# Splitting weights in pairs, combining from PSUM, and scaling O later: one transformer block on one core

## The chip, the core and the metric

The kernel runs on one core of a Trainium2 chip. A core has a matrix engine (PE; its weight loads are shown as PEld), a vector engine (DVE), a scalar engine (ACT) and GpSimd (POOL). They run at the same time, each working through its own queue in order, and wait for each other by semaphores. SyncE (SP) does no arithmetic; its queue issues the transfers between the core's memory (SBUF) and the chip's memory (HBM), which 16 DMA engines carry out. PE writes to PSUM, eight banks of 128 x 512 float32 values; DVE and ACT read and write PSUM and SBUF, POOL only SBUF.

The metric is the device time of one execution in microseconds (us). The time before is the median of three runs. The profile is that of one execution, with a time of its own.

## The reference

One block: a layer norm scaled and shifted by a condition c, attention of 32 query heads over a cache of 16 key/value heads, of which only the last 512 positions count, an output projection, a second such norm, and a gated feed-forward network. 2048 tokens of width 576, head size 128, hidden size 4608, all float32.

```python
mod = (_silu(c) @ w_mod).reshape(c.shape[0], 6, 1, -1)
sa, ca, ga, sb, cb, gb = (mod[:, 0], mod[:, 1], mod[:, 2], mod[:, 3], mod[:, 4], mod[:, 5])
h = _layernorm(x, axis=-1) * (1 + ca) + sa
x = x + ga * _A_ref(h, A_k_cache, A_v_cache, A_wq, A_wo)
h = _layernorm(x, axis=-1) * (1 + cb) + sb
x = x + gb * _B_ref(h, B_w_gate, B_w_up, B_w_down)
...
q = (lambda x, *d: x.transpose(*d))((x @ wq).reshape(B, Sq, Hq, Dh), 0, 2, 1, 3)
scores = jnp.einsum("bhqd,bhkd->bhqk", q, k) * (Dh ** -0.5)
p = _softmax(scores, axis=-1)
o = jnp.einsum("bhqk,bhkd->bhqd", p, v)
```

## The kernel before

**Split numbers.** A float32 value v is kept as hi, a rounded form that PE takes (fp32r), and lo = v - hi. ACT makes hi by a copy, DVE or POOL subtracts to get lo. A matrix product is then three: hi times hi, hi times lo and lo times hi.

**Seven products for eight.** The big projections use the Strassen-Winograd scheme. x and the weights are cut into four quarters each, and combinations of quarters enter seven products. In the code the weight's factors are A11, A12, A22, S1, S2, S4, S3 and the activation's B11, B21, T1, T2, B22, T3, T4; product (u, A11) multiplies A11 by B11, A12 by B21, S1 by T1, S2 by T2, S4 by B22, S3 by T3 and A22 by T4.

**The Q phase.** The 2048 tokens are four blocks of 512. A pair of blocks (0 and 1, then 2 and 3) is the one halving of the scheme; the 576 input rows give the other (288 rows: two chunks of 128 and one of 32), and heads are taken two at a time. There are 32 units u: u 0 to 15 take the heads in order for blocks 0 and 1, u 16 to 31 again for blocks 2 and 3. Each unit has seven products, so the phase has 224 steps; `order` lists them, `place` gives a product's step, and step numbers begin at NLO = -224, so that attention begins at 0. One product is seven matmuls of 512 columns (`q_product`): for each 128-row chunk hi by hi, lo by hi and hi by lo, and one matmul for the 32-row chunk, which keeps hi and lo on different partitions.

The schedule is by step: `at_n(step, fn)` puts work before the step's product and `at_late` behind it. Each engine executes its own work in the order in which the program lists it.

- Weights: `load_raw(u)` fetches the four quarters of a unit into one of two RAW tiles (five transfers). `w_sums` has POOL form S1, S2, S4 and S3. `w_split` makes hi (ACT, 128 x 384) and lo (DVE, once 128 x 256 and once 32 x 128) of one factor, into one of nine `sw` tiles.
- First products: products A11 and A12 need only block 0. So for the first EARLY = 8 units these come ahead of everything, in the phase's first 16 steps, with their own loads (`load_first`) and splits (`w_split_first`); the A11 products are kept in `first_room`, tiles of blocks 2 and 3 that are not loaded yet. Meanwhile block 1 goes through its norm and the combinations T1 to T4 are made (`first_sum`, `chunk_split`). The early units' other five products follow unit by unit, and load the raw weights again.
- Outputs: each unit gives four tiles of 128 x 512, scaled by QSCALE, in one of four `qo` tiles, stored to HBM by SP (`q_store`). Sums of products are built in PSUM where the order allows; otherwise DVE adds a kept product (`q_out` with add). PSUM banks: a (two), b (one), c (one), st (four).
- The pair switch: while units 8 to 15 run, blocks 2 and 3 are loaded and normalised, transposed by PE (`turn`), copied with gain and shift (`third_out`), combined (`third_sum`), and kept in float32. When the last product of unit 15 with an old factor is issued, `convert` splits the new one into the same tile.
- Background work: `SPANS` and the planner loop behind it place jobs that prepare the later weights ("ab": load, four sums on POOL, store; "tail": load, sums, splits, 24 stores; "wo" and "down" likewise) in rooms that are free in certain steps. They run through the Q phase and attention.

**Attention.** 128 blocks b of four steps; each step handles 128 queries: scores (three matmuls; DVE takes the row maximum, `neg`), exponentials on ACT (`pp`), four transposes (`pt`), hi and lo of the transposed P (`ptt`, ACT and DVE), and three matmuls with V (`pv`, bank `ot`, two banks). The sums of a block's exponentials are inverted (`rs`), and since a row is needed that holds them along the free axis on every partition, they go through HBM: `put_rs` writes rs to rscr (2 KB), `get_rs` reads it back to all partitions as `rb` (256 KB), with SP waiting for the write to land. In step 4b+8, when the last matmul of the block's pv is issued, DVE multiplies O by rb into `ov`. `put_o` stores it two steps later; for some heads POOL first forms sums of O (`sum_o`, `put_sx`, `sum_last`).

After attention come the output projection and the feed-forward network, which the change leaves as they are.

Of the kernel before, what the change touches and what calls it, by code (L numbers as in the profile page):

```python
# [44 lines left out]
def adaln_block_kernel(ctx: ExitStack, tc: tile.TileContext, x, k_cache, v_cache, wq, wo, w_gate, w_up, w_down,  # L45
# [65 lines left out]
    def sw_tile(shape, dt=F32R):  # L111
        return qw.tile(shape, dt, tag="sw", name="sw", bufs=9)
# [125 lines left out]
    QC = {}  # L238

    def q_room(c):  # L240
        QC[c] = wp.tile([P, 5, BLK], F32R, tag=f"hc{c}", name="qc", bufs=1)

    def q_places(c, s):
        r, to = (slice(0, P), 3 + s) if s < 2 else (slice(TQ, 2 * TQ), 2)
        return r, QC[c][:, s, :], QC[c][r, to, :]

    def q_hi(c, s, v, k=None):
        hi = q_places(c, s)[1]
        if k is None:
            nc.scalar.activation(hi, v, AF.Copy)  # L250
        else:
            nc.scalar.activation(hi, v, AF.Identity, bias=scol[:, k : k + 1])

    def q_lo(c, s, v, eng, k=None):
        r, hi, lo = q_places(c, s)
        if k is None:
            eng.tensor_sub(lo, v[r], f32(hi[r]))
        else:
            eng.scalar_tensor_tensor(lo, v[r], scol[r, k : k + 1], f32(hi[r]), op0=OP.add, op1=OP.subtract)
# [26 lines left out]
    EARLY = 8  # L286
    wqh = wq.rearrange("(h r) n -> r h n", h=2)

    def load_raw(u):
        raw, n0 = RAW[u % 2], u % HKV * 2 * P  # L290
# [17 lines left out]
    def raw_of(u, a):  # L308
        return RAW[u % 2][:, :, {A11: 0, A21: 1, A12: 2, A22: 3}[a], :]

    def w_sums(u, which):
        for a in which:
            WS[u, a] = qw.tile([P, 3, P], F32, tag="ws", name="ws", bufs=5)
            eng = nc.gpsimd
            if a == S1:
                eng.tensor_add(WS[u, a], raw_of(u, A21), raw_of(u, A22))
            elif a == S2:
                eng.tensor_sub(WS[u, a], WS[u, S1], raw_of(u, A11))
            elif a == S3:
                eng.tensor_sub(WS[u, a], raw_of(u, A11), raw_of(u, A21))  # L320
            else:
                eng.tensor_sub(WS[u, a], raw_of(u, A12), WS[u, S2])

    def w_split(u, a, src=None):
        if src is None:
            src = raw_of(u, a) if (u, a) not in WS else WS[u, a]
        t = SWQ[u, a] = sw_tile([P, 5, P])
        nc.scalar.activation(t[:, 0:3, :], src, AF.Copy)
        nc.vector.tensor_sub(t[:, 3:5, :], src[:, 0:2], f32(t[:, 0:2, :]))
# [1496 lines left out]
```

## Time and profile before

| | |
|---|---|
| median of three runs | 3252.54 us (3252.29 to 3254.05) |
| the profiled execution | 3254.14 us, span 3252.3 us |
| mean granted clock of PE | 0.974 |
| moved by the DMA engines | 635.14 MB, 195 GB/s on average |

A profile row names line, engine and operation, then out<-in by the program's tile names, the shape, the count, the busy time, the mean time of one in ns, and the engine's idle time just before, with what ended it. All instructions have line L36 here, that of a helper through which every operation passes, so one goes by tile names: `a`, `b`, `c`, `st`, `pt` and `ot` are PSUM banks, `qc` the split activations of the Q phase, `sw` split weights, `ws` their sums, `raw` raw weights, `x` the blocks or whatever background work uses their room. `a<-qc,sw` is a matmul of a Q product. A window's row gives its length, the busy time of PE, PEld, DVE, ACT and POOL with counts, the granted clock as a fraction of full speed, the mean busy share of the DMA engines, and GB/s. In a list of waits, "A <- B: 131.9, 47, 7.8" means that A stood idle 131.9 us in all, 47 times, 7.8 us at the longest, until B was done. SPq is the queue of SP.

### The profile page before, as it was taken

Reading aid. Unit: us, or ns where it says so; the run is one execution under the profiler, and the core shown is the slowest. Engines: PE = TensorE matmul, PEld = TensorE weight load, DVE = VectorE, ACT = ScalarE, POOL = GpSimd, SP = SyncE. Lnnn points to the kernel's source line nnn. Section 1 sums busy time; section 2 is a strip of 40 time slices with the busy share of each in tenths; the row PEclk is TensorE's granted clock in tenths of the full one; section 3 lists DMA queues with packets and bytes.
Section 4 is the critical chain, followed back from the end, with each engine's and each line's share of the span. In section 5 each row is a group of like instructions: output and inputs, shape, how many; then the busy total and the mean of one; then the engine's idle time right before and its main releaser. Section 6 shows DMA issues by size and latency. Waiting matters only on the chain.

```text
span 3252.3 us, 50928 instructions
## 1 busy us (share of the span) xinstructions
PE 3023.0 (93%) x16375; PEld 2579.5 (79%) x16375; DVE 2323.0 (71%) x4113; ACT 1814.1 (56%) x3727; POOL 1846.8 (57%) x1680
## 2 busy tenths in 40 slices
PE   7897988788898889888999999999999999999999
PEld 5676776677777767667799999888888888888888
DVE  7878766676777767666878877766666686666667
ACT  5255446677777777666744465544444454444443
POOL 2645654577787777432155521776655565656555
PEclk9999998999999999999999999999999999999999
DMA  4664887888788877788644766655555565555554
GB/s 145 217 201 151 254 238 200 226 235 233 231 252 265 257 239 238 203 209 239 203 153 176 273 228 236 181 158 153 159 174 140 153 200 157 145 143 139 149 140 119
DMA packets 505386, 635.14 MB, mean 195 GB/s; under 512 B 55712, under 2 KB 425120, under 8 KB 496416
## 3 DMA queue, kind: packets, MB, share of 16 engines
q1 hardware_dynamic: 503984, 631.36, 65.0%
q8 instruction: 131, 2.15, 0.3%
q14 instruction: 135, 1.11, 0.1%
q10 hardware_dynamic: 1136, 0.53, 0.1%
HBM read 424.48 MB, written 207.25 MB: 194 GB/s over the span
## 4 chain that ended last, share of the span: by engine, by line
PE 58%; DMA 10%; issue 4%; DVE 3%; POOL 3%; SPq 2%; ACT 2%; DVEq 0%; POOLq 0%; ACTq 0%
PE a L36 19%; PE w L36 12%; PE c L36 10%; PE st L36 5%; PE b L36 5%; PE ot L36 5%; DMA rb<-rscr 4%; DMA rscr<-rs 4%; PE pt L36 3%; SPq L36 2%; DVE ptt L36 1%; POOL x L36 1%; DVE neg L36 1%; ACT pp L36 1%; POOL qt L36 1%
## 5 line engine op out<-in xcount | busy, mean ns | idle before, releaser
L36 DVE TENSOR_TENSOR x<-w,x 128x288 f32<-128x288 f32 x964 | 417.2, 451 | 233.5 <-PE w L36 231.3
L36 PE MATMUL a<-hc,sw 128*128 128x512 f32 x2016 | 580.4, 393 | 1.5 <-DVE v L36 1.4
L36 PE MATMUL st<-kt,qt 128*128 128x512 f32 x1536 | 504.6, 438 | 1.1 <-POOL qt L36 1.1
L36 DVE TENSOR_TENSOR ptt<-pt,ptt 128x512 fp32r<-128x512 f32 x512 | 351.6, 687 | 152.9 <-ACT ptt L36 152.1
L36 ACT ACTIVATE pp<-st,neg 128x512 f32<-128x512 f32 x512 | 352.1, 688 | 191.3 <-DVE neg L36 190.2
L36 PE MATMUL ot<-ptt,vs 128*128 128x512 f32 x1536 | 453.3, 404 | 4.8 <-DVE ptt L36 4.3
L36 PE MATMUL pt<-ident,pp 128*128 128x128 f32 x2048 | 323.3, 282 | 130.1 <-DVE ptt L36 125.4
L36 PEld LDWEIGHTS pt<-ident,pp 128*128 128x128 f32 x2048 | 260.2, 145 | 220.9 <-issue 126.4
L36 PEld LDWEIGHTS a<-hc,sw 128*128 128x128 f32 x2016 | 355.1, 188 | 41.5 <-DVE v L36 3.3
L36 POOL TENSOR_TENSOR qt<-qr,qt 128x512 fp32r<-128x512 f32 x128 | 165.5, 1293 | 371.7 <-ACT qt L36 354.1
L36 ACT ACTIVATE ptt<-pt 128x512 fp32r<-128x512 f32 x512 | 304.8, 595 | 115.4 <-PE pt L36 113.2
L36 ACT ACTIVATE sw<-sr 128x384 fp32r<-128x384 f32 x504 | 257.5, 518 | 188.3 <-issue 88.0
L36 PEld LDWEIGHTS ot<-ptt,vs 128*128 128x128 f32 x1536 | 296.4, 194 | 82.3 <-DVE ptt L36 12.9
L36 DVE TENSOR_REDUCE neg<-st 128x1 f32<-128x512 f32 x512 | 347.5, 679 | 2.7 <-PE st L36 2.7
L36 POOL TENSOR_TENSOR sw<-sr,sw 128x256 fp32r<-128x256 f32 x245 | 185.1, 756 | 275.4 <-ACT sw L36 256.9
L36 PEld LDWEIGHTS w<-wh,hl 128*128 128x128 f32 x1776 | 297.4, 188 | 53.2 <-DVE x L36 5.7
L36 PE MATMUL w<-wh,hl 128*128 128x288 f32 x1776 | 326.3, 295 | 3.0 <-DVE x L36 2.9
L36 PE MATMUL c<-hc,sw 128*128 128x512 f32 x1008 | 302.4, 393 | 0.0
L36 DVE TENSOR_TENSOR sw<-sr,sw 128x256 fp32r<-128x256 f32 x259 | 189.1, 731 | 142.7 <-ACT sw L36 140.0
L36 PEld LDWEIGHTS st<-kt,qt 128*128 128x128 f32 x1536 | 263.1, 198 | 28.0 <-POOL qt L36 2.1
L36 PE MATMUL a<-qc,sw 128*128 128x512 f32 (+1 forms) x912 | 238.4, 407 | 46.1 <-DVE qo L36 28.3
L36 POOL TENSOR_TENSOR hl<-vs,hl 128x512 fp32r<-128x512 f32 x139 | 192.0, 1382 | 107.7 <-ACT hl L36 104.3
(267 smaller groups left out, 5897.1 us busy)
## 6 DMA issues: line engine op xcount, KB each, us to landing
sr<-wsc SPq DMA_DIRECT2D x504, 192.0 KB
wh<-dsc SPq DMA_DIRECT2D x144, 288.0 KB
qscr<-qo SPq DMA_DIRECT2D x128, 256.0 KB
qr<-qscr SPq DMA_DIRECT2D x128, 256.0 KB
vr<-oscr SPq DMA_DIRECT2D x32, 1024.0 KB
rb<-rscr SPq DMA_DIRECT2D x126, 256.0 KB
oscr<-ov SPq DMA_DIRECT2D x63, 512.0 KB
wsc<-x SPq DMA_DIRECT2D x26, 896.0 KB
```

Source lines behind the costliest of these rows:

```text
L36: i = got(*args, **kw)
```

## The change

- Two factors are split at a time. `sw` tiles are twice as wide and there are four; A22, the odd one, has a tile of its own (`sa`). `w_sums` writes a pair into one `ws` tile. One ACT copy of 768 columns takes the place of two of 384, one DVE subtraction of 512 that of two of 256, one of 32 x 256 that of two of 32 x 128. For the first products of units 1 to 13 POOL does this last one.
- EARLY is 14: 28 first products instead of 16. Six more units need rooms for A11's product: attention's `kt` and `qr` tiles, idle in this phase. The first product A12 of odd units uses bank c.
- For early units the kept product is copied by ACT into PSUM before S1's product, so that S2's adds to it there; the kept copies that DVE made with an add are now plain ACT copies, as in later units, and the last output is copied by ACT.
- QSCALE moves from the outputs to K (`prep_k`).
- Combinations from PSUM: blocks 1, 2 and 3 are transposed without the gain; DVE forms gain times the PSUM tile minus a kept tile (`chunk_from`) for T1, T2 and T3; T4 is still a subtraction on POOL. The shift enters at the split, as a bias (`bias_of`, with `dcol` the difference of the two halves' shifts). The scaling of block 1's rows by DVE (`ln_scale`) goes.
- The pair switch: norm of block 2 in steps 50 to 67, of block 3 in 71 to 84, turns in 85 to 96. The second pair's B11 and T1 are split into attention's idle tiles (`kt`, `qt`, `pp`) in steps 93 to 101; the other five take over tiles of used factors of the first pair (`OLD`) in steps 104 to 113, a third at a time.
- Background work may use the rooms of blocks 0 and 1 from step 27 to 83 (before: 24 to 82) and again from 116 (before: 118).
- Attention: `get_rs` is issued one step later, O is multiplied at the end of step 4b+10 instead of within 4b+8 (`ov_out`), and the stores and sums of O move two steps with it.

```diff
     def sw_tile(shape, dt=F32R):
-        return qw.tile(shape, dt, tag="sw", name="sw", bufs=9)
+        return qw.tile(shape, dt, tag="sw", name="sw", bufs=4)
...
-    EARLY = 8
+    EARLY = 14
...
+    def w_sums(u, k):
+        t = WS[u, k] = qw.tile([P, 3, 2, P], F32, tag="ws", name="ws", bufs=2)
+        eng = nc.gpsimd
+        if k == 0:
+            eng.tensor_add(t[:, :, 0], raw_of(u, A21), raw_of(u, A22))
+            eng.tensor_sub(t[:, :, 1], t[:, :, 0], raw_of(u, A11))
...
+    def w_split(u, names, src, tail=None):
+        tail = tail or nc.vector
+        n = len(names)
+        t = sw_tile([P, 5, 2, P]) if n == 2 else qw.tile([P, 5, 1, P], F32R, tag="sa", name="sa", bufs=2)
+        nc.scalar.activation(t[:, 0:3], src, AF.Copy)
+        nc.vector.tensor_sub(t[:, 3:5], src[:, 0:2], f32(t[:, 0:2]))
+        r = slice(2 * TQ, 3 * TQ)
+        tail.tensor_sub(t[r, 2], src[r, 2], f32(t[r, 2]))
...
+    def w_split_first(u):
+        w_split(u, (A11, A12), RAW[u // 2 % 2][:, :, u % 2 :: 2, :], nc.gpsimd if u else None)
...
     def first_room(u):
-        return bg_view(2 + u // 4, (u % 4) * BLK, [BLK])
+        if u < 8:
+            return bg_view(2 + u // 4, (u % 4) * BLK, [BLK])
+        return P1K[u // 2 % 2][:, u % 2] if u < 12 else P1Q[u % 2]
...
             if first:
-                p = ps_b()
+                p = ps_c() if u % 2 else ps_b()
...
-            q_product(u, S1, T1, PC[u], True)
-            v = KEEP[u, S1] = mod_rows("gate1")[:, :BLK]
-            if first:
-                nc.vector.scalar_tensor_tensor(v, PC[u], QSCALE, first_room(u), op0=OP.mult, op1=OP.add)
-            else:
-                nc.scalar.activation(v, PC[u], AF.Copy, scale=QSCALE)
...
             if first:
                 PA[u] = ps_a()
+                nc.scalar.activation(PA[u], first_room(u), AF.Copy)
+            q_product(u, S1, T1, PC[u], True)
+            KEEP[u, S1] = mod_rows("gate1")[:, :BLK]
+            nc.scalar.activation(KEEP[u, S1], PC[u], AF.Copy)
...
+    def chunk_from(d, h, s, p, y):
+        nc.vector.scalar_tensor_tensor(CH[d, s], p, gain_of(h, s), CH[y, s], op0=OP.mult, op1=OP.subtract)
...
+    OLD = {B21: B11, T2: T1, B22: B21, T3: T2, T4: B22}
+
+    def convert(c, s):
+        if s == 0 and c in (B11, T1):
+            ts = [at.tile([P, 2, BLK], F32R, tag="kt" if c == B11 else "qt", name="qk", bufs=2) for _ in range(2)]
+            tail = at.tile([P, BLK], F32R, tag="pp", name="qk", bufs=2)
+            QC[1][c] = [ts[0][:, 0], ts[0][:, 1], tail[:, :], ts[1][:, 0], ts[1][:, 1]]
+        elif s == 0:
+            q_room(1, c, OLD[c])
...
+    for c, k in ((B11, 93), (T1, 98), (B21, 104), (T2, 106), (B22, 108), (T3, 110), (T4, 112)):
         for s in range(3):
-            q_hi(c, s, CH[c, s])
-            q_lo(c, s, CH[c, s], nc.gpsimd if s == 1 else nc.vector)
...
+            at_late(n + k + s // 2 + (s if c in (B11, T1) else 0), convert, c, s)
...
             if b < NBLK - 2:
                 at_late(n - 1, put_rs, b)
-                at_late(n + 1, get_rs, b)
+                at_late(n + 2, get_rs, b)
...
         if k == KT - 1:
...
+            if b < NBLK - 2:
+                at_late(TPB * b + 10, ov_out, b)
+            else:
+                ov_out(b)
```

More of the change, by code (lines that the diff above doesn't have):

```diff
@@ L530, in adaln_block_kernel @@
     place = {x_: q_n(i) for i, x_ in enumerate(order)}
[L531 to L533 removed]
+    for u in range(2, EARLY):
+        at_n(max(place[u, A11] - 3, q_n(0)), w_split_first, u)
         if u >= 4:
```

394 lines of the change are left out of this document (187 added, 207 removed).

## The prediction

> **What bounds the kernel now.** I read the page first (busy shares, chain), then the stages in windows, then who waits for whom in the two stages that the change touches, then single instructions.
>
> ```profile
> span 3252.3 us, 50928 instructions
> PE 3023.0 (93%) x16375; PEld 2579.5 (79%) x16375; DVE 2323.0 (71%) x4113; ACT 1814.1 (56%) x3727; POOL 1846.8 (57%) x1680
> PE 58%; DMA 10%; issue 4%; DVE 3%; POOL 3%; SPq 2%; ACT 2%; DVEq 0%; POOLq 0%; ACTq 0%
> PE a L36 19%; PE w L36 12%; PE c L36 10%; PE st L36 5%; PE b L36 5%; PE ot L36 5%; DMA rb<-rscr 4%; DMA rscr<-rs 4%; PE pt L36 3%; SPq L36 2%; DVE ptt L36 1%; POOL x L36 1%; DVE neg L36 1%; ACT pp L36 1%; POOL qt L36 1%
> ```
>
> PE leads, but 8% of the chain is two tiny DMAs of attention: a block's reciprocal sums go out (rscr<-rs) and come back spread over the partitions (rb<-rscr). The stages (length, busy times, granted clock, DMA share, GB/s):
>
> ```profile
> 22.90:104.50 81.60, 56.87 (x226) 41.81 (x227) 69.75 (x132) 41.16 (x78) 33.28 (x30) 0.92 0.36 110
> 104.50:215.00 110.50, 96.66 (x394) 75.57 (x392) 94.96 (x187) 37.72 (x76) 59.46 (x65) 0.95 0.80 241
> 215.00:296.80 81.80, 65.76 (x286) 50.68 (x287) 67.97 (x96) 51.67 (x99) 44.99 (x40) 0.96 0.31 106
> 296.80:492.50 195.70, 178.20 (x753) 142.80 (x753) 143.35 (x243) 91.18 (x187) 111.23 (x123) 0.97 0.83 248
> 492.50:660.00 167.50, 136.86 (x683) 109.69 (x682) 106.77 (x175) 112.55 (x261) 86.08 (x93) 0.92 0.77 215
> 660.00:1250.00 590.00, 523.70 (x2713) 420.53 (x2712) 416.96 (x679) 436.44 (x956) 462.46 (x360) 0.96 0.81 244
> 1250.00:1430.00 180.00, 153.82 (x792) 124.63 (x791) 122.19 (x199) 115.00 (x265) 81.30 (x86) 0.93 0.80 224
> 1430.00:1560.00 130.00, 110.43 (x558) 89.66 (x558) 87.11 (x142) 81.64 (x190) 38.37 (x42) 0.91 0.78 212
> 1560.00:1645.00 85.00, 83.84 (x455) 68.36 (x453) 72.66 (x117) 63.73 (x148) 18.73 (x15) 1.00 0.58 177
> 1645.00:3252.00 1607.00, 1597.02 (x9431) 1439.67 (x9429) 1130.01 (x2111) 774.76 (x1457) 906.13 (x820) 1.00 0.56 170
> ```
>
> The first four rows are the Q phase, cut at its products 28, 84 and 118 of 224; the next five are attention; the last is untouched. How fast each goes undisturbed:
>
> ```profile
> 486.17 1.75 PE L36 MATMUL c<-qc,sw 128*128 128x512 f32 x7
> 487.76 1.75 PE L36 MATMUL a<-qc,sw 128*128 128x512 f32 x7
> ...
> 1560.08 0.60 PE L36 MATMUL pt<-ident,pp 128*128 128x128 f32 x4
> ...
> 1561.91 0.60 PE L36 MATMUL pt<-ident,pp 128*128 128x128 f32 x4
> ```
>
> A product of seven matmuls takes 1.59 us, an attention step 1.83. So 224 products would take 356 us where the phase takes 469.6, and 512 steps 937 us where attention takes 1152. Some 110 and 210 us are lost; the last stage, 1597 of 1607 busy, loses nothing.
>
> ```profile
> DVE ov L36 <- DMA rb<-rscr: 131.9, 47, 7.8
> ...
> PE pt L36 <- DVE ptt L36: 125.4, 51, 8.1
> ...
> SPq L36 <- DMA rscr<-rs: 261.0, 94, 5.9
> ```
>
> In attention DVE stands 131.9 us before the multiplication of O (ov) until rb has come; its split of the transposed P (ptt) is queued behind, and PE waits 125.4 us for that. SP waits 261.0 us in 94 places for the sums to land before it may fetch them, and all other transfers wait behind it. One such place:
>
> ```profile
> 1535.72 6.84 SPq L36 DMA_DIRECT2D wsc<-x  x12
> 1542.61 0.45 SPq L36 DMA_DIRECT2D rb<-rscr  x1
> ...
> 516.07 1.06 DVE L36 TENSOR_TENSOR ov<-ot,rb 128x512 f32<-128x512 f32 x1 [2.39 <-DMA rb<-rscr]
> ...
> 1547.28 1.05 DVE L36 TENSOR_TENSOR ov<-ot,rb 128x512 f32<-128x512 f32 x1 [7.77 <-DMA rb<-rscr]
> ```
>
> Twelve background stores sit before the fetch; O waits 7.77 us (the last of the 47 waits; the first is the 2.39).
>
> **Attention, worked out.** O's multiplication moves from the middle of step 4b+8 to the end of 4b+10: 2.4 steps, 4.4 us. The fetch moves one step, 1.83 us, past whatever SP has in that step: usually one or two issues, in a burst six stores of 0.57 = 3.4 us. Against the fetch O gains 2.6 us as a rule, 4.4 if SP was blocked anyhow (part of its 261.0 us is hidden by the extra step), 1.0 in a burst. Cutting each of the 47 waits by 1.0, 2.6 or 4.4 leaves 89, 40 or 10 us of the 131.9. I take 2.6, since bursts and blocked places about balance: 92 us go. PE follows at 125.4/131.9, so 87 us.
>
> With the gaps goes part of the slow clock: length times (1 - granted clock) is 13 + 24 + 13 + 12 = 61 us in the four disturbed rows and none in the fifth, which has no such wait. In proportion, 61 x 87/125 = 43 us. [...]
>
> Against this stands traffic. The long row moves 244 GB/s at a share of 0.81, so 301 GB/s would fill the engines; 68 us less there makes the share 0.92. Transfers then land later, and loads for the background work, waited for by POOL and ACT in order, begin to show. I give back 30 us of the 130. Attention: **-100**, bounds -30 (cut 1.0, and the same price) and -176 (cut 4.4, all the clock, no price).
>
> O's store and the sums on POOL move two steps with it; no one waits for them soon. The ot banks and rb buffers (two each) are now held until three steps, 5.5 us, before block b+2 needs them: free of cost unless O is late by more. Folding the scale into K adds nothing: one ACT copy and one DVE operation with PSUM input, as before.
>
> **Q phase, worked out.** The rows of operations (columns: busy us, mean ns, idle before):
>
> ```profile
> L36 DVE TENSOR_TENSOR sw<-ws,sw 128x256 fp32r<-128x256 f32 x128 | 77.6, 606 | 16.2 <-ACT sw L36 14.0
> ...
> L36 DVE TENSOR_TENSOR sw<-ws,sw 32x128 fp32r<-32x128 f32 x128 | 67.0, 523 | 3.3
> L36 ACT ACTIVATE sw<-ws 128x384 fp32r<-128x384 f32 x128 | 66.1, 518 | 43.7 <-POOL ws L36 39.8 <-PE a L36 2.4 <-PE c L36 1.6
> ...
> L36 DVE TENSOR_TENSOR qc<-x,qc 128x512 fp32r<-128x512 f32 x9 | 10.7, 1195 | 1.5 <-ACT qc L36 1.3
> ...
> L36 ACT ACTIVATE qt<-qr 128x512 fp32r<-128x512 f32 x9 | 5.7, 631 | 0.0
> ...
> L36 DVE SCALAR_TENSOR_TENSOR gate<-c,x 128x512 f32<-128x512 f32 x8 | 5.5, 691 | 2.7 <-PE c L36 2.6
> ```
>
> Two splits cost DVE 2 x (606 + 523) = 2258 ns. A pair is not in the trace: its 512-wide part lies between 691 (the last row, whose input from PSUM keeps it off POOL's way) and 1195 (nine with both inputs in SBUF), its 256-wide tail at 606: 1297 to 1801, saving 0.46 to 0.96 us; I take 0.7, the middle, as POOL works half the time in these stages. With 96 pairs that is 67 us (44 to 92). [...]
>
> On ACT a 768-wide copy, by the slope from 518 to 631, costs 857 ns: 2 x 518 - 857 is 0.18, 17 us in all. For the eight early units three DVE adds of 0.69 each become ACT copies, and one output of six more units goes from ACT to DVE: DVE -12, ACT about +19 with the preloads of PSUM, each 0.6 and needed two products (3.2 us) later, so hidden by S1's product. ACT is busy 41 to 63% of these rows, so it stays clear of the path; POOL gets 13 tails and as many sums as before.
>
> Fourteen early units instead of eight add 6 x 5 loads of raw weights to SP, by their shapes 6 x 0.36 = 2.2 MB. Rooms and gains that only change their place cost nothing: the rooms are read long before block 2 or the background work fills them, and the six transposes of the gains fit beside the first products. Stage by stage:
>
> ```profile
> 38.14 4.83 SPq L36 DMA_DIRECT2D raw<-in_A_wq_dram  x10
> ...
> PE b L36 <- DVE qo L36: 12.5, 3, 8.9
> ...
> SPq L36 <- DVE sw L36: 34.3, 13, 12.1
> ...
> PE a L36 <- DVE qo L36: 8.0, 3, 4.5
> ...
> PE a L36 <- DVE qo L36: 16.8, 9, 7.7
> ```
>
> *Products 0 to 27* (first three rows): the one b bank waits for a DVE that is busy 69.75 of 81.6 us with block 1's combinations, and SP's loads wait for DVE's splits; now these spread over 28 first products instead of 16, and odd units use the c bank. Floor 28 x 1.59 + 2.7 for six turns of transposes (each as two matmuls, 0.45, an estimate) = 47, ceiling today's 82; ten raw loads per four products hold SP 4.83 of 6.4 us with stores still to come, so I take 61: -20. *Products 28 to 83*: floor 89, but a unit takes five products here, not seven, for longer: traffic of 56/5 = 11.2 units instead of 28/5 + 28/7 = 9.6. By its shapes a unit loads 0.72 MB and stores 1.05, so 2.8 MB, or 9 us at 301 GB/s, come beside the 88 us (0.80 of 110.5) that DMA has; at a share of 0.93 that is 104: -7. *Products 84 to 117* (fourth row), the pair switch: floor 34 x 1.59 + 12 x 0.45 = 60, DVE 68 of 81.8. Layer norm of blocks 2 and 3 is spread out earlier, combinations come straight from PSUM (0.69 each for operations of 1.2), and two go early into attention's idle tiles; the wait for reused slots is 7 products or more. I take 64: -18. *Products 118 to 223* (last row): the same loads and stores, two steps earlier; its waits are outputs whose stores sit behind background transfers. I take 0. Q phase: **-45**, bounds 0 and -80 (all floors). First split, tile reuse at attention's start: at most one product, 1.6 us, left out.
>
> **Sum.** The profiled run took 3254.1 us (span 3252.3), 1.6 above the median, so the sums compare as they are: 3254 - 100 - 45 = **3109**.
>
> **Rivals.**
> *A, transfers take the wait's place.* At full pace the background work's loads and stores are late and POOL and ACT stop instead. For: shares of 0.77 to 0.81 already. Against: the row at 1560 keeps pace. Attention gives 30: 3179.
> *B, the early Q stages gain nothing*, since SP's extra loads or DMA bound them as DVE does now: 3154.
> *C, slower.* The fetch, moved behind another step's issues, loses more than O gains. It decides at 4.4 us of slip; if each of the 47 waits met a burst like the 6.84 us above, each would grow by 2.44, 115 us, less Q's 45: 3324. Against: such bursts are few.
> *D, it does not do what it says*: SP is serial, rb is late by as much as O moves, and DVE's saving lies off the path: 3254.
> *E, all at the floors*: 3254 - 176 + 30 - 80 = 3028.
>
> **Chances.** Forecast 0.60 (its own range 3040 to 3175, by the bounds of 0.46 and 0.96 and of the cuts), A 0.15, B 0.10, C 0.05, D 0.05, E 0.05. Faster holds forecast, A, B and E: 0.90; same D: 0.05; slower C: 0.05, where a change of 0.2% (6.5 us) is about what a measurement of this kernel can tell. The range takes in A and B with their spread and leaves out C, D, E: 3035 to 3215.
>
> **What would show it.** Right: DVE's wait for rb near 40 us, PE's wait for ptt near 40 and SP's for rscr halved; granted clock 0.98 in attention; the 28th product near 84 us, the 118th near 252 and attention's start near 448. Wrong: a wait of POOL or ACT for background loads (A), of PE for SP's raw weights (B), of PE for ot banks (C).

## The result, and the profile after

The changed kernel takes 3193.78 us (median of four runs, 3193.25 to 3195.46) where the kernel before took 3252.47: a ratio of 0.9819 (95% interval 0.9802 to 0.9836), 59 us less. The forecast of 3109 us expected 145 less; the time lies 19 us above the forecast's own range (3040 to 3175). The page of the profiled execution (3193.45 us):

```profile
span 3191.5 us, 50573 instructions
PE 3014.5 (94%) x16375; PEld 2567.4 (80%) x16375; DVE 2251.4 (71%) x3908; ACT 1818.9 (57%) x3663; POOL 1854.6 (58%) x1685
PE 63%; DMA 12%; DVE 7%; ACT 5%; issue 4%; POOL 4%; SPq 3%; ACTq 0%; POOLq 0%; DVEq 0%
PE a L36 22%; PE w L36 12%; PE c L36 11%; PE b L36 6%; PE ot L36 5%; PE st L36 4%; SPq L36 3%; DMA rb<-rscr 3%; PE pt L36 3%; DMA rscr<-rs 2%; DVE sw L36 2%; ACT pp L36 1%; ACT ptt L36 1%; DMA raw<-in_A_wq_dram 1%; POOL x L36 1%
```

The two small DMAs have 5% of the chain instead of 8%; DVE's weight splits (sw) and the raw weights' transfers, which were not named before, now stand among the fifteen named. The stages, cut at the same products as before (length, busy times, granted clock, DMA share, GB/s; four rows of the Q phase, five of attention, the rest):

```profile
23.20:88.60 65.40, 55.74 (x226) 40.69 (x226) 49.62 (x80) 39.33 (x65) 32.29 (x30) 0.95 0.44 133
88.60:203.30 114.70, 97.67 (x392) 74.94 (x393) 79.05 (x137) 52.05 (x86) 73.25 (x77) 0.96 0.82 249
203.30:284.40 81.10, 67.55 (x288) 52.14 (x287) 56.78 (x81) 49.72 (x82) 34.72 (x32) 0.94 0.33 108
284.40:492.30 207.90, 185.67 (x756) 145.43 (x755) 111.28 (x154) 86.81 (x143) 120.05 (x127) 0.94 0.82 243
492.30:644.40 152.10, 126.53 (x649) 101.28 (x648) 101.31 (x167) 108.64 (x252) 83.88 (x89) 0.93 0.79 222
644.40:1173.40 529.00, 489.44 (x2604) 395.25 (x2602) 403.13 (x651) 416.17 (x916) 438.13 (x342) 0.98 0.85 262
1173.40:1382.10 208.70, 184.82 (x973) 149.91 (x973) 152.24 (x244) 144.62 (x330) 109.71 (x107) 0.96 0.84 230
1382.10:1480.00 97.90, 90.57 (x481) 74.19 (x480) 74.55 (x121) 68.56 (x160) 33.17 (x36) 0.97 0.73 192
1480.00:1577.30 97.30, 91.64 (x486) 74.77 (x484) 81.56 (x128) 69.34 (x159) 21.83 (x17) 0.97 0.71 229
1577.30:3191.00 1613.70, 1606.28 (x9435) 1444.03 (x9433) 1130.07 (x2112) 775.11 (x1458) 902.83 (x819) 1.00 0.56 169
```

| us | before | after | forecast |
|---|---|---|---|
| products 0 to 27 | 81.6 | 65.4 | 61 |
| 28 to 83 | 110.5 | 114.7 | 104 |
| 84 to 117 | 81.8 | 81.1 | 64 |
| 118 to 223 | 195.7 | 207.9 | 196 |
| attention | 1152 | 1085 | 1052 |
| the rest | 1607 | 1614 | 1607 |

What the first stage gained the second and the fourth gave back, so the Q phase gained nothing; attention gained 67; the untouched rest lost 7. Yet DVE did save what was forecast. Operations of the pair splits, by shape:

```profile
L36 DVE TENSOR_TENSOR sw<-ws,sw 128x512 fp32r<-128x512 f32 x64 | 53.1, 830 | 53.2 <-ACT sw L36 53.1
L36 DVE TENSOR_TENSOR sw<-ws,sw 32x256 fp32r<-32x256 f32 x64 | 44.4, 693 | 1.4
```

These 64 pairs of sums take 830 + 693 = 1523 ns each instead of 2258, 0.74 us less (forecast 0.7); the 32 pairs straight from raw weights take 901 + 717. The DVE column of the first four rows sums to 297 us, before to 376. In attention (list of waits between its first and last transpose of P):

```profile
PE ot L36 <- DVE ptt L36: 56.0, 34, 8.1
DVE ov L36 <- DMA rb<-rscr: 35.2, 16, 8.3
PE pt L36 <- DVE rs L36: 17.9, 3, 10.4
DVE ov L36 <- DMA oscr<-ov: 12.8, 5, 5.5
PE pt L36 <- DVE ptt L36: 5.0, 6, 3.3
```

O's wait for rb fell from 131.9 to 35.2 us (forecast 40), but PE still waits 56.0 + 17.9 + 5.0 = 79 us for DVE, where 40 were forecast. Two more points went otherwise: SP's wait for the sums to land fell from 261.0 to 222.9 us, not to half, and O's wait for the store of an earlier output (oscr<-ov), at which the forecast saw no one wait, grew from 3.1 to 12.8.

### The profile page after: what moved, and what is told of

Its sections match the earlier page's. It is cut to its first block, busy times and chain, and to the rows that moved or that the text cites. A ratio compares the mean times of both kernels' runs of the same rounds, so it can differ in the third digit from the quotient of the medians.

```text
span 3191.5 us, 50573 instructions
## 1 busy us (share of the span) xinstructions
PE 3014.5 (94%) x16375; PEld 2567.4 (80%) x16375; DVE 2251.4 (71%) x3908; ACT 1818.9 (57%) x3663; POOL 1854.6 (58%) x1685
## 4 chain that ended last, share of the span: by engine, by line
PE 63%; DMA 12%; DVE 7%; ACT 5%; issue 4%; POOL 4%; SPq 3%; ACTq 0%; POOLq 0%; DVEq 0%
PE a L36 22%; PE w L36 12%; PE c L36 11%; PE b L36 6%; PE ot L36 5%; PE st L36 4%; SPq L36 3%; DMA rb<-rscr 3%; PE pt L36 3%; DMA rscr<-rs 2%; DVE sw L36 2%; ACT pp L36 1%; ACT ptt L36 1%; DMA raw<-in_A_wq_dram 1%; POOL x L36 1%
## 5 line engine op out<-in xcount | busy, mean ns | idle before, releaser
L36 PE MATMUL st<-kt,qt 128*128 128x512 f32 x1536 | 493.3, 430 | 3.0 <-POOL qt L36 3.0
L36 PEld LDWEIGHTS ot<-ptt,vs 128*128 128x128 f32 x1536 | 289.4, 192 | 143.6 <-DVE ptt L36 78.7
L36 PE MATMUL pt<-ident,pp 128*128 128x128 f32 x2048 | 313.5, 276 | 26.8 <-DVE rs L36 17.9
L36 PEld LDWEIGHTS st<-kt,qt 128*128 128x128 f32 x1536 | 256.4, 193 | 29.0 <-POOL qt L36 3.6
L36 POOL TENSOR_TENSOR x<-x 128x256 f32<-128x256 f32 (+3 forms) x226 | 178.1, 805 | 74.4 <-DMA x<-in_B_w_up_dram 45.9
```

Of the source, the lines that this page charges most:

```text
L36: i = got(*args, **kw)
```

## The experiments

Beside the experiments the kernel before took 3234.6 to 3237.4 us, so ratios are compared, and stages with the run *sw_apart*, whose instructions and time are those of the changed kernel. When a product, attention (first and last transpose of P) and the execution begin or end, in us, read from each run's trace:

| run | ratio to before (95%) | product 28 | 84 | 118 | attention | end |
|---|---|---|---|---|---|---|
| att_only | 0.9817 (0.9799-0.9836) | 104.7 | 217.7 | 301.0 | 496.0-1568.8 | 3177.8 |
| q_only | 0.9967 (0.9954-0.9980) | 88.8 | 205.0 | 284.0 | 490.5-1607.8 | 3223.6 |
| halves | 0.9880 (0.9862-0.9898) | 90.9 | 209.2 | 293.9 | 508.2-1584.5 | 3200.9 |
| sw_apart | 0.9822 (0.9807-0.9836) | 88.4 | 201.1 | 282.1 | 486.4-1558.9 | 3175.0 |
| col64 | 0.9825 (0.9805-0.9845) | 88.5 | 202.7 | 283.4 | 488.5-1560.1 | 3171.2 |
| shift32 | 1.0007 (0.9998-1.0017) | 105.1 | 214.8 | 296.6 | 494.6-1617.3 | 3236.1 |
| act_first | 0.9797 (0.9781-0.9813) | 83.8 | 197.5 | 268.8 | 473.7-1555.6 | 3171.7 |
| raw_early | 0.9863 (0.9848-0.9878) | 90.8 | 214.0 | 293.5 | 500.1-1575.0 | 3190.4 |
| early12 | 0.9834 (0.9809-0.9859) | 94.3 | 210.6 | 290.0 | 495.4-1565.8 | 3181.5 |
| gate_dve | 0.9815 (0.9786-0.9845) | 88.6 | 202.8 | 283.5 | 488.0-1563.7 | 3180.1 |
| half_raw | 0.9792 (0.9775-0.9810) | 88.8 | 196.1 | 277.4 | 482.8-1550.6 | 3166.9 |
| get_back | 0.9856 (0.9835-0.9876) | 88.5 | 203.8 | 283.2 | 488.2-1570.1 | 3186.4 |
| rb_old | 0.9770 (0.9756-0.9785) | 88.3 | 202.4 | 281.8 | 489.2-1542.6 | 3158.2 |
| spread | 0.9772 (0.9758-0.9787) | 89.5 | 200.3 | 281.6 | 481.8-1542.0 | 3158.8 |
| before_spread | 0.9926 (0.9899-0.9953) | 104.9 | 214.5 | 295.0 | 487.9-1604.2 | 3214.1 |
| act_spread | 0.9733 (0.9718-0.9748) | 83.8 | 195.2 | 267.0 | 465.2-1531.7 | 3147.1 |
| best | 0.9718 (0.9688-0.9748) | 83.6 | 193.8 | 265.6 | 463.2-1529.3 | 3140.9 |
| best_wm | 0.9666 (0.9648-0.9683) | 83.5 | 194.7 | 266.0 | 465.3-1514.4 | 3125.7 |

### The two parts apart

*att_only* is the kernel before with attention's part of the change, *q_only* the changed kernel without it. The two main lines (O's stores and sums move with them):

```diff
-                at_late(n + 1, get_rs, b)
+                at_late(n + 2, get_rs, b)
...
+                at_late(TPB * b + 10, ov_out, b)
```

> The kernel before with the attention part alone (fetch of rb one step later, O multiplied at the end of step 4b+10, O's stores and sums two steps later); the Q phase is that of before. Theory 1 (the two parts do not touch each other, and the whole gain is attention's 1152 to 1085 us): 3252.5 - 67 = about 3186, between 3180 and 3190, below the changed kernel. Rival (attention gains only because the Q phase hands over something, the scale folded into K or rooms that come free two steps earlier): less than 40 us of gain, above 3212. In its Q phase the matmuls of a product should follow each other by 227 ns if the 234 of the changed kernel belong to its code, and the stage behind attention should take 1607.

> The changed kernel with attention's part undone: the fetch of rb, the product with O and the stores are where they were before. Theory 1 (parts independent, Q phase gains nothing): 3193.8 + 67 = about 3260, slower than before by 0 to 8 us (the last stage's 6.6 us too, if they belong to the Q part). Rival (the Q phase does gain, and the gain is lost in attention to traffic): 3215 to 3240. The step that the prediction used (Q phase -45) asks for 3208.

Attention's part alone gives the whole gain (0.9817 against 0.9819). The Q part alone gives 0.3%, some 11 us: attention begins 5.5 us earlier than in *att_only*, its last stage is 7 longer, and its attention of 1117 cannot be set against before's, which was not profiled beside it. The two ratios multiply to 0.9785, so together the parts give some 11 us less than one by one. The intervals (5 to 6 us each way) leave that figure rough, and no run says where it goes.

### Is the saved DVE time on the path?

*halves* splits each pair as two single factors again:

```diff
-        nc.scalar.activation(t[:, 0:3], src, AF.Copy)
-        nc.vector.tensor_sub(t[:, 3:5], src[:, 0:2], f32(t[:, 0:2]))
+        for i in range(n):
+            nc.scalar.activation(t[:, 0:3, i], src[:, :, i], AF.Copy)
+            nc.vector.tensor_sub(t[:, 3:5, i], src[:, 0:2, i], f32(t[:, 0:2, i]))
...
```

> The changed kernel with every pair of factors split as two single ones again (two ACT copies of 384 and four DVE or POOL subtractions instead of one and two), in the same tiles at the same steps. It gives DVE back some 67 us and ACT 17. The prediction's step (DVE's time in the splits is on PE's path in the first three stages) asks for a Q phase longer by 30 to 60: 3224 to 3254. Rival (the saved DVE time lies beside the path): 3194 to 3204.

Between the two: DVE is busy 52 us longer in the Q phase than in *sw_apart* (349 instead of 297), ACT 9 (237 instead of 228); the phase ends 22 us later, and the kernel is 0.6% longer. So some two fifths of what the pairs save is on PE's path, ACT's small share included, which the run does not take apart. By stage it is 3, 6, 4 and 10 us, most of it where the forecast had none (118 to 223) and least where it had most (0 to 27).

### Where the pair switch lost its gain

In the changed kernel, around product 96 (233.03), the one timeline of all engines has:

```profile
231.80 0.69 ACT L36 ACTIVATE x<-st,gcol 128x512 f32<-128x512 f32 x1 [1.99 <-DVE x L36]
232.38 0.59 ACT L36 ACTIVATE gate<-a 128x512 f32<-128x512 f32 x1
...
233.03 1.22 PE L36 MATMUL a<-qc,sw 128*128 128x512 f32 x2 [3.39 <-ACT gate L36]
```

ACT copies the transposed tile (x<-st) only when DVE has formed its combination of the same tile; the copy to gate stands behind it, and PE waits for that. The wait is one of the program's own: ACT's copy waits for the semaphore that DVE's combination raises, and with the order turned round (*act_first*, below) DVE's waits for the one that ACT's copy raises. Why the program puts two readers of a tile in order, no run shows. In products 84 to 117 of *sw_apart*:

```profile
ACT x L36 <- DVE x L36: 12.5, 5, 3.5
...
ACT hs L36 <- DVE x L36: 1.5, 1, 1.5
```

*act_first* swaps the two lines, there and for `half_second`:

```diff
-        chunk_from(T1, 0, s, p, B11)
         chunk_copy("B12", s, p, gain_of(0, s))
+        chunk_from(T1, 0, s, p, B11)
...
```

> The changed kernel with two lines swapped twice: of a transposed tile in PSUM the copy by ACT is issued ahead of the combination by DVE, not behind it. Theory (at the pair switch ACT stands behind DVE at each of these tiles, 1.5 to 3.5 us at a time, and PE waits for what ACT has queued behind, such as the copy to gate): products 84 to 117 in 72 to 77 instead of 79 to 81, first stage 1 to 3 us less, in all 5 to 10 us less than the changed kernel. Rival (the chain through DVE is as long either way, or DVE then stands behind ACT): within 3 us of the changed kernel, ratio 0.982.

This wait is gone from ACT's list, and the stage's row goes from the first to the second:

```profile
201.00:282.10 81.10, 67.57 (x288) 52.12 (x288) 56.78 (x80) 49.76 (x82) 34.73 (x32) 0.94 0.32 109
```

```profile
197.40:268.80 71.40, 63.84 (x287) 50.20 (x287) 57.81 (x78) 49.93 (x82) 35.11 (x32) 0.98 0.37 124
```

With the first stage's 60.5 instead of 65.2, the Q phase is 13 us shorter, the kernel 0.25% (its attention was 9 longer in the profiled execution). Of the 10 us at the pair switch PE's busy time, at a clock of 0.98 instead of 0.94, makes some 4. The engines do the same work; only the order of two readers of one PSUM tile differs.

### Why products 28 to 83 gained nothing

The longest stop of PE there, at product 82 in the changed kernel (SP's, DVE's and PE's timelines):

```profile
175.50 4.04 SPq L36 DMA_DIRECT2D wsc<-x  x7
179.64 0.60 SPq L36 DMA_DIRECT2D qscr<-qo  x1
180.29 1.05 SPq L36 DMA_DIRECT2D x<-in_A_x_dram  x1
181.38 4.46 SPq L36 DMA_DIRECT2D wsc<-x  x6
185.91 2.42 SPq L36 DMA_DIRECT2D raw<-in_A_wq_dram  x5
```

```profile
194.77 1.85 DVE L36 TENSOR_TENSOR sw<-ws,sw 128x512 fp32r<-128x512 f32 x2 [6.58 <-ACT sw L36]
```

```profile
198.42 1.19 PE L36 MATMUL c<-qc,sw 128*128 128x512 f32 x2 [7.52 <-DVE ln_v L36]
```

The background tail's stores (wsc<-x, 24 in four steps) hold SP; raw weights are issued late, their sums and splits come late, PE stops 7.52 us. (The releaser is named ln_v because a few small DVE operations stand between the split and PE.) Four runs ask how far this goes.

*raw_early* fetches earlier, and splits A22, the tile's last reader, earlier:

```diff
-            at_n(n - 8, load_raw, u)
-            times = (n - 4, n - 3), (n - 2, n), n + 1
+            at_n(max(n - 11, q_n(2 * EARLY - 4)) if u else n - 8, load_raw, u)
+            times = (n - 4, n - 3), (n - 2, n), n - 2
```

> The changed kernel with the raw weights of the fourteen early units fetched three steps earlier (n-11 instead of n-8); the split of A22, the last reader of a RAW tile, moves from n+1 to n-2 to make that possible. Theory (a unit of five products leaves SP too little time behind the background stores, and the late raw weights stop PE, as at product 82 for 7.5 us): products 28 to 83 in 104 to 108 instead of 112 to 115, no such stop at product 82, 6 to 10 us less than the changed kernel. Rival (the DMA engines themselves are full there and the time goes elsewhere): 3194 at the chip of before's 3252, that is ratio 0.982.

A miss: the stage is 10.6 us longer (123.2 against 112.6). SP reaches the fetch before the tile is free and stands there (its wait for DVE's sa in this stage goes from 9.4 to 21.9 us) with the outputs' stores behind it. PE's wait for DVE's outputs at the c bank grows from 8.9 to 20.1 us, at nearly every unit; whether SP's standing or the earlier split of A22 does that, the run does not separate. An earlier place in a queue was no gain here, where the thing it waits for was not early too.

*early12* sets `EARLY = 12` (here units 10 and 11 make their first two products with unit 0's weights, whose fetch now comes ahead of their split); *gate_dve* gives the copy of S1's product to DVE:

```diff
-            nc.scalar.activation(KEEP[u, S1], PC[u], AF.Copy)
+            (nc.vector.tensor_copy(KEEP[u, S1], PC[u]) if first else nc.scalar.activation(KEEP[u, S1], PC[u], AF.Copy))
```

> The changed kernel with twelve early units instead of fourteen: four first products fewer, two units more with seven products instead of five. Theory (units of five products ask for raw weights, sums and stores faster than SP and the DMA engines bring them): fewer of them in products 28 to 83, the point of product 84 reached 3 to 8 us earlier than 201 to 204, kernel 3 to 8 us less. Rival (their number does not matter, each unit loses the same in its own queues): point of product 84 and kernel within 3 us, ratio 0.982.

> The changed kernel with the copy of S1's product to gate1 made by DVE instead of ACT for the fourteen early units. Theory (ACT waits 30 us for the c bank at this copy, the weight splits queue behind it, DVE and PE wait for those): ACT's wait for c goes from 30 to under 5 us in products 28 to 83, that stage takes 103 to 108 instead of 112 to 115, kernel 5 to 10 us less. Rival (ACT's waiting is slack, and DVE then stands in ACT's place): stage 111 to 116, kernel within 4 us, ratio 0.982.

Both theories fall. Fewer early units make product 84 later (210.6), not earlier. ACT's 30 us of waiting for bank c turn into 37 for bank a, and the stage takes 114.2.

*half_raw* leaves six fetches out:

```diff
-            at_n(n - 8, load_raw, u)
+            if u % 2 == 0 or u < 2:
+                at_n(n - 8, load_raw, u)
```

> The changed kernel without the fetch of raw weights for units 3, 5, 7, 9, 11 and 13: their sums and splits read what the tile held before, all else is done as it was. 30 of SP's issues and 4.3 MB less in products 28 to 83. Theory (SP and the DMA engines bring raw weights too late for units of five products): point of product 84 at 190 to 196 instead of 201 to 204, no stop of 7 us at product 82, kernel 6 to 14 us less. Rival (the chain of PE, ACT and DVE through the one c bank sets the pace, about 1 us a unit, and the late weights hide behind it): point of product 84 at 199 to 204, kernel within 4 us.

```profile
88.80:196.10 107.30, 97.56 (x392) 74.59 (x393) 79.95 (x138) 51.84 (x86) 71.54 (x75) 0.97 0.73 225
```

107.3 us, at the border of the two: the stop at product 82 shrinks to 2.1 us. So some 5 us belong to these six fetches, whose issues and traffic went together (the share fell to 0.73); the kernel is 10 us shorter (0.9792), as the theory asked, but half of that lies behind the stage. The other 18 us above the forecast's floor of 89 stay. In the changed kernel PE stops 0.6 to 1.7 us at most units' S1, mostly for DVE's output from the one c bank; what would shorten that was not tried.

### Attention: what is still late

In the changed kernel, near O's longest wait (SP's timeline, then DVE's):

```profile
1249.93 7.83 SPq L36 DMA_DIRECT2D wsc<-xr  x13
1257.86 1.59 SPq L36 DMA_DIRECT2D rb<-rscr  x1
...
1264.99 0.34 SPq L36 DMA_DIRECT2D rb<-rscr  x1
```

```profile
1264.79 1.05 DVE L36 TENSOR_TENSOR ov<-ot,rb 128x512 f32<-128x512 f32 x1 [8.28 <-DMA rb<-rscr]
```

A burst again: 13 stores hold SP 7.83 us, the fetch is issued at 1257.86, and its data end O's wait at 1264.79, 6.9 us later. In these 6.9 us the DMA engines' share is 0.88. *get_back* undoes the fetch's step, *rb_old* lets it read sums that landed long ago (those of three blocks earlier, with eight rscr tiles instead of four):

```diff
-                at_late(n + 2, get_rs, b)
+                at_late(n + 1, get_rs, b)
...
-        keep_order(nc.sync.dma_start(RB[b], rscr[b % 4].rearrange("p t -> (p t)").partition_broadcast(P)))
+        keep_order(nc.sync.dma_start(RB[b], rscr[(b if b < 3 else b - 3) % 8].rearrange("p t -> (p t)").partition_broadcast(P)))
```

> The changed kernel with the fetch of rb issued at its old step, O still scaled at the end of 4b+10. The prediction's step says that O gained 4.4 us and gave 1.83 back by the later fetch: then the waits of O for rb fall from 25-35 us to about 10 and attention gains up to 20. Rival (the later fetch was what took SP's waiting for the sums away; with the old step SP stands 260 us before the fetch again and everything queued behind it is late): within 5 us of the changed kernel or slower by 5 to 15, with SP's wait for rscr back at 250 to 260.

> The changed kernel with eight rscr tiles instead of four, and the fetch of rb reading the sums of three blocks earlier (its own for the first three blocks), written some 20 us before: the fetch has nothing to wait for, and O is scaled by another block's sums. Theory (what attention still loses to DVE, 67 us of PE's gaps here, is rb coming late): the waits of O for rb go to near 0, PE's gaps from 86-92 to 30-45, attention from 1072-1082 to 1010-1030. Rival A (the transfers themselves are the limit now, they only wait elsewhere): gaps of POOL and ACT loads grow, attention above 1055. Rival B (half of it is O's own store not yet out, oscr, or DVE's load): 1040 to 1055.

With the fetch at its old step O waits no less (23.1 us against 25.0), SP's wait for the sums is back at 255.1 (198.3 in *sw_apart*), and the kernel is 0.3% longer: the later step pays by freeing SP. With old sums SP's wait falls to 6.5 us, and attention to 1053, 19 us less: short of the 1010 to 1030 expected, and in rival B's range. In attention of *sw_apart*, then of *rb_old*:

```profile
PE ot L36 <- DVE ptt L36: 47.5, 33, 6.0
DVE ov L36 <- DMA rb<-rscr: 25.0, 11, 6.7
```

```profile
PE ot L36 <- DVE ptt L36: 37.1, 33, 4.6
DVE ov L36 <- DMA rb<-rscr: 18.0, 8, 5.0
```

O still waits 18.0 us for rb although its sums landed long before. What is left, then, is the place of the fetch behind SP's other issues, or the transfer's own time; these runs do not part the two. *spread* puts the tail's stores two steps apart (and holds their room three steps longer), *before_spread* does so in the kernel before, *act_spread* adds the swap of *act_first*:

```diff
-            at_n(n + (9 if kind == "ab" else 16 if kind == "tail" else 16) + part, bg_store, k, part)
+            at_n(n + (9 if kind == "ab" else 16) + 2 * part, bg_store, k, part)
```

> The changed kernel with the background tail's 24 stores put in every second step instead of every step (its room held 25 steps instead of 22, so the planner's jobs shift a little). Theory (in the Q phase the long stops of PE, 7.5 us at product 82, 4 at 161, 8 at 194, 3 to 4 at 223, come from SP being held by these stores while raw weights and outputs queue behind): products 28 to 83 in 105 to 109, 118 to 223 in 190 to 195, Q phase 12 to 18 us less, kernel 8 to 18 us less. Rival (DMA traffic as such is the limit): stops stay or move, kernel within 4 us of the changed one.

> The kernel before with the background tail's 24 stores in every second step instead of every step, as in the run spread. Theory (SP's bursts cost both kernels, so that part of the wait for rb that the prediction charged to O's place belongs to them): 10 to 25 us less than before, most of it in attention, O's wait for rb from 98-110 to 70-90. Rival (only the changed kernel suffers from them, since there the fetch is one step later and moved past them): within 5 us of before.

> The changed kernel with both edits: ACT's copies ahead of DVE's combinations (10 us less by itself) and the tail's stores in every second step. Theory: both gains add, ratio to before 0.974 to 0.977. Rival (the stores' spacing gives nothing): 0.9797 as with the first edit alone.

The size was right (0.5% for the changed kernel, 0.7% for the one before), the place mostly wrong: of 16 us in *spread* 5 are in the Q phase, where the stops at products 161 and 194 move to 166 and 196 (4.5 and 5.6 us instead of 4.1 and 8.3) and that at product 82 falls from 6.7 to 3.6, and 12 in attention. In *before_spread* O's wait for rb did not fall (123 us; 98 in *shift32* with the old spacing), so there the gain is not through rb; what it is through stays open. The two edits together give more than expected.

*best* is *act_spread* with a longer dcol (*col64*, below). In it PE's gaps in attention are 81 us, and of those with DVE as releaser, 20 us in five places have no multiplication of O among DVE's last five instructions. ACT's, then PE's lines in attention of *best*:

```profile
ACT wm L36 <- DMA wm<-in_w_mod_dram: 19.2, 6, 5.5
...
PE pt L36 <- DVE ptt L36: 14.9, 5, 6.4
...
PE pt L36 <- DVE rs L36: 6.1, 2, 5.9
```

ACT stands for the modulation weights with the copies of P queued behind. *best_wm* lets their sums begin four steps later:

```diff
-            at_n(n + 3 + c, lambda m, c: mod_sum(wm[m], c), m, c)
+            at_n(n + 7 + c, lambda m, c: mod_sum(wm[m], c), m, c)
...
```

> The changed kernel with the three edits that shortened some stage: ACT's copies ahead of DVE's combinations, the tail's stores in every second step, and dcol of 64 bytes a partition. Theory: the first two give 0.9733 as before, and the third takes 5 us off the last stage: ratio 0.9715 to 0.9725. Rival (the third gives nothing in sum): 0.9733.

> The kernel of run best with the four modulation weights' sums on ACT and POOL four steps later behind their fetch (n+7 and n+13 instead of n+3 and n+9). Theory (ACT stands for these loads, with the copies of P queued behind it, so PE's long gaps near 570, 631, 678 and 690 us are theirs): PE's gaps in attention from 81 to 55-65, 15 to 30 us less than best, ratio to before 0.963 to 0.967. Rival (the gaps are bursts of SP that hit whatever comes next): 0.972 as best.

The first line is gone (0.2 us), the next two have become

```profile
PE pt L36 <- DVE ptt L36: 5.0, 5, 3.2
```

and attention takes 1049 instead of 1066. PE's gaps fell to 70 us, short of the 55 to 65 expected; the 20 us are 4. At 0.9666, 3129 us beside a before of 3234.6, this version is faster than both kernels.

## Why the forecast was wrong

The sum was 85 us short: 45 in the Q phase, 33 in attention, 7 in the last stage. Rival B (nothing from the early Q stages) came nearest in the Q phase, but by other waits in part: B was to come from SP's extra loads or the DMA engines.

**DVE's saving** (-67, with others -79): right in size (DVE's splits of weights take 183 us instead of 256, with 13 tails gone to POOL), though by two errors that cancel: the 512-wide part took 830 ns, below the middle of 691 and 1195, and the tail 693 where 606 was assumed. Operations with both inputs in SBUF are longer beside POOL's work, and those with one from PSUM are not, in the trace of before: of DVE's 128 x 512 operations v<-v,g took 680 ns on average where POOL was idle throughout (33 of them) and 1289 where it worked for at least half of the operation (38); ptt<-pt,ptt, with `pt` in PSUM, took 685 and 688. The changed kernel's 512-wide part took 685 in the first case (26) and 974 in the second (31). That the saving lies on the path of the first three stages was wrong for most of it: of 52 us of DVE's time in the whole phase *halves* shows 12 there, and 10 in the fourth stage.

**Products 0 to 27** (-20): 16 came, and 21 with *act_first*, at 60.5 us for a forecast of 61. The pair splits give only 3 us of it (*halves*). What remains for the rest is the spreading over 28 products and two banks, which no run took out by itself.

**84 to 117** (-18): this step failed. "Combinations come straight from PSUM (0.69 each for operations of 1.2)" counts only DVE's time. The same tile has a second reader, ACT, issued behind; its queue now stood behind DVE at each of the six tiles that both read. Without that, 10 of the 18 come. The rest is two stops of about 3 us at products 105 and 112, where DVE's outputs stand behind its splits.

**28 to 83** (-7): the stage took 4 us more. The price of traffic was argued from the DMA engines' share, which stayed at 0.82 (before 0.80) where 0.93 was reckoned with. The runs show 5 us from late raw weights (*half_raw*); *spread*, with the same traffic, nearly halved the stop at product 82, so the burst in SP's queue is at least a part of it. The other 18 us above the floor are open.

**118 to 223** (0): "the same loads and stores" was wrong. The stage is 12 us longer in the result, 9 longer in *sw_apart* than in *att_only*, and some 5 of the 9 are one new stop before the last product, with a slow product behind it. In *sw_apart* (SP's, DVE's and PE's timelines):

```profile
469.38 8.02 SPq L36 DMA_DIRECT2D wsc<-x  x12
477.49 0.39 SPq L36 DMA_DIRECT2D qscr<-qo  x1
...
480.01 0.69 DVE L36 TENSOR_TENSOR qo<-a,gate 128x512 f32<-128x512 f32 x1 [4.93 <-DMA qscr<-qo]
...
480.76 1.65 PE L36 MATMUL a<-qc,sa 128*128 128x512 f32 x3 [4.14 <-DVE qo L36]
```

Twelve background stores sit before an output's store, DVE stands 4.93 us until that has landed, and PE 4.14 for DVE. *att_only* has no stop there, and with the stores two steps apart it is gone (*spread*). The remaining 4 us are open.

**Attention** (-100): O's waits were cut as said. The step that failed is "PE follows at 125.4/131.9": O's waits for rb fell by 97 us, PE's waits for DVE by 51. Of PE's waits before, 23 us in 21 places (after: 22 in 6) had no O among DVE's last five instructions, so no cut of O's waits could end them; those after belong mostly to the modulation weights (*best_wm*). And what is left of O's waits costs PE nearly all that it costs DVE: 99 us of PE stood behind 138 of O's before, 47 behind 49 after. Besides, 21 short stops (10 us) now stand behind an O that came in time, before 3 (8.5 us). PE's gaps in attention fell from 144 to 102 us, not by 87. The clock's part was 26 us instead of 43: length times (1 - clock) is now 11 + 11 + 8 + 3 + 3 = 35. The 30 given back for traffic happened to cover part of the error. Rival A's sign is there in part: POOL's waits for transfers in attention grew from 9 to 68 us (45 in *sw_apart*), ACT's stayed at 31. The runs show two things that hold attention now, bursts of stores (12 us, *spread*) and ACT's stops for the modulation weights (17, *best_wm*); whether a fetch is late in SP's queue or in busy DMA engines they do not separate.

**The rest** (0): +7, explained below. Rival C did not occur; moved past SP's bursts, the fetch still won.

## What to carry to other kernels

When two engines read the same PSUM tile, look at who is issued first: if the program orders the readers, as here, the second one's whole queue waits with it (12.5 us of ACT's at the pair switch), and a saving on the first can turn into a wait on the second. Before a wait's cost is cut in proportion, sort the waits by length and by what stands next to them: here the many short ones went, and the few long ones behind a burst of issues stayed and cost the most. A queue of small stores is worth taking apart in time: that alone gave 0.5% and 0.7% on the two kernels here.

## What the runs showed of the hardware

**Addresses.** The change adds a tile, dcol, of 12 bytes a partition, ahead of qc and most tiles of the last stage, so these begin further on in memory: by 32 bytes in the programs as built, where the lowest `qc` tile begins at byte 76032 of a partition instead of 76000 (76064 in *col64*, 76032 in *shift32*). No trace shows addresses. Products follow each other by 1.59 us before (486.17 to 487.76) and by 1.63 after (PE's timeline, starts in the first column):

```profile
185.83 1.79 PE L36 MATMUL a<-qc,sw 128*128 128x512 f32 x7
187.46 1.79 PE L36 MATMUL c<-qc,sw 128*128 128x512 f32 x7
```

Three runs: *sw_apart* keeps the pair's two factors apart in their tile, *col64* makes dcol longer, *shift32* gives the kernel before a tile that no one reads:

```diff
-        t = sw_tile([P, 5, 2, P]) if n == 2 else
+        t = sw_tile([P, 2, 5, P]).rearrange("p n k d -> p k n d") if n == 2 else
...
-    dcol = const.tile([P, 3], F32, name="dcol")
+    dcol = const.tile([P, 16], F32, name="dcol")
...
+    pad = const.tile([P, 3], F32, name="pad")
```

> The changed kernel with the pair's two factors each in one piece of the tile (2 x 5 x 128 instead of 5 x 2 x 128), so that a factor's hi and lo lie as they did before; instructions and their counts are the same. Theory (the interleaved weights make a matmul follow the one before by 234 ns instead of 227): Q phase shorter by 10 us, 3184. Rival (the 7 ns have nothing to do with the layout): 3194 +- 4, spacing still 234.

> The changed kernel with one tile made longer: dcol (the difference of the two halves' shifts) is 16 columns instead of 3, 64 bytes a partition instead of 12 (which take 32). Nothing else differs, but every tile laid out behind it (qc of the Q phase, the tiles of the last stage) stands 32 bytes further on, so that its address is 32 modulo 64 as before the change, not 0. Theory (the address modulo 64 of the tiles that PE streams sets the spacing of matmuls, 234 or 227 ns, and the 6.6 us of the last stage): Q phase shorter by about 10, the last stage 1609 instead of 1616, together 12 to 18 us less than the changed kernel, ratio to before 0.977. Rival (the spacing comes from something else in the code, such as the order of instructions): no change, ratio 0.982, spacing 234.

> The kernel before with one unused tile of 12 bytes a partition (and a memset of it) beside gcol, which moves the same tiles by 32 bytes the other way. Theory: spacing 234 in the Q phase, the last stage 1616 instead of 1609, 12 to 18 us slower than before (ratio 1.004 to 1.006). Rival: ratio 1.000, spacing 227.

The layout of the weights does nothing (*sw_apart*: ratio 0.9822, spacing 234 ns). With 32 bytes more (*col64*) the median spacing of matmuls goes from 234 to 231 ns; with 32 bytes added to the kernel before (*shift32*) from 227 to 234. The last stage in *sw_apart*, *col64*, *att_only* (the old addresses) and *shift32*:

```profile
1558.90:3175.00 1616.10, 1608.23 (x9440) 1445.43 (x9438) 1132.32 (x2114) 776.07 (x1459) 904.30 (x820) 1.00 0.55 169
```

```profile
1560.10:3171.20 1611.10, 1603.64 (x9439) 1443.60 (x9438) 1119.26 (x2114) 775.91 (x1459) 919.57 (x820) 1.00 0.56 170
```

```profile
1568.80:3177.70 1608.90, 1599.79 (x9439) 1441.66 (x9437) 1128.11 (x2114) 776.22 (x1459) 907.20 (x820) 1.00 0.55 170
```

```profile
1617.30:3236.10 1618.80, 1609.24 (x9441) 1446.11 (x9439) 1132.88 (x2115) 775.66 (x1459) 905.99 (x820) 1.00 0.56 169
```

The other runs agree: from the last transpose of P to the end it is 1615 to 1617 us in the thirteen that have the changed kernel's layout, 1609 to 1610 in the three with that of before, 1611 to 1612 in the three with the longer dcol. So 32 bytes are worth 5 to 10 us where PE is busy throughout, and nothing that shows in the Q phase (463.2 us from product 0 to attention in *sw_apart*, 465.4 in *col64*), which is not paced by PE. In sum they are below what a run can tell (ratios of 0.9825 and 1.0007). *col64* comes only about half way back, so the place modulo 64 bytes, on which the runs were planned, is not the whole of it. Why the address matters is not shown.

**The clock after a stop.** In products 118 to 223 of all runs there are 134 stops of PE of 0.3 to 2.5 us before a product, and all but two are followed by one at full pace (1.87 to 1.91 us from the start of its first matmul to the end of its last). After 2.7 to 3.4 us the product takes 2.2 to 3.4 us, and after 3.7 us or more 3.1 to 3.4, with matmuls 427 ns apart instead of 227 or 234. (In the changed kernel the product at 429.82 us takes 3.35 us after a stop of 8.39.) That is also why the forecast's proportional cut of the clock's loss was too large: in attention the stops over 2.8 us fell from 19 to 12 only.
